# GEGLU feed-forward on one core: leading weights on one queue in 2 KB rows, later x behind chunk 5, chunks 6 and 7 by halves

## Chip, cores and metric

The kernel runs on one core of one Trainium2 chip. The metric is the device time of one execution in microseconds (us). Before the change three runs gave 299.56, 300.29 and 300.46 us, median 300.29.

## What is computed

From the reference, with x of 32 x 32 x 1024, w_gate and w_up of 1024 x 3584 and w_down of 3584 x 1024, all bf16:

```python
def _gelu(x):
    return jax.nn.gelu(x, approximate=True)
...
def reference(x, w_gate, w_up, w_down):
    return (_gelu(x @ w_gate) * (x @ w_up)) @ w_down
```

x is 1024 tokens of 1024 features. The first two products contract over features, the third over the 3584 hidden units.

## The kernel before

**Tiles and stages.** TensorE multiplies 128 x 128 weight tiles by up to 512 columns. The 1024 features are eight chunks of 128 (index k or dk), the hidden units 28 blocks of 128 (index m). A "part" is one block m for one range of tokens, with a gate sum G and an up sum U in PSUM, which has eight banks. Stage one makes all parts: TensorE sums G and U over the eight chunks (`part_step`, L362 to 392), ScalarE takes the gelu of G into a small buffer (L441, one of four), VectorE multiplies it by U into hT (L474; these multiplies are called E0, E1 and so on, by part). Stage two multiplies hT by w_down (L422), and ScalarE and VectorE by turns copy the result out, SyncE (SP) stores it.

**The start.** Weights and x come in together, and x has to be turned so that features lie on partitions. Tokens 0 to 255 (XA) arrive as two slices xa of 128 tokens, one on SP's queue and one on ScalarE's (L295). TensorE turns them by multiplying with an identity (`turn_xa`, L349 to 360; the identity is made on POOL, L319) into banks 3 to 7; four copies on VectorE and one on ScalarE (`xa_copy`, L302 to 307; `XA_PS` on L130 gives bank and chunks, `XA_ACT` on L131 the copies that are ScalarE's) bring them to xT. Tokens 256 to 1023 come later in three pieces: XB1 (128 tokens), XB2 (128) and XC2 (512) (`load_x`, L282 to 287; each piece by two queues, two transfers each, in 512-byte rows). VectorE turns them with its own transposes (L465): A0 to A7 are chunks of XB1, B of XB2, D of both together, C of XC2.

**Leading weights.** Blocks 0 to 7 of w_gate and w_up, 1024 columns, are needed first. `W0` (L134 to 136) cuts them: chunks 0 and 1 in two halves of 512 columns (1 KB rows), chunks 2 to 5 whole (2 KB rows), chunks 6 and 7 as a pair in two halves of 512 columns (1 KB rows). w_gate goes through SP's queue and w_up through ScalarE's (`early_loads`, L294 to 300), each behind its slice of xa and ahead of its half of later x. ScalarE makes its one xa copy after the ninth step of its issues (`ACT_EARLY`, L132). Each transfer has its own semaphore.

**The order by hand.** TensorE's order is a list of steps. `together` goes chunk by chunk over several parts, `one_by_one` finishes a part before the next; a step waits for its weights, for its bank to be free, for its xa copies or transposes. Parts 0 to 7 (blocks 0 to 7, tokens 0 to 255) and 8 to 15 (tokens 256 to 511) share a bank for G and U, so that ScalarE waits for U. The list at the start:

```python
together(range(0, 4), 0, 2)
together(range(4, 8), 0, 2)
together(range(0, 8), 2, 6)
one_by_one(range(0, 8), 6)
together(range(8, 12), 0, 4, XB1)
```

VectorE's order is the string `mix` (L190): multiplies E and transposes A to D. Part 8 reuses bank 0 and needs E0, part 11 needs E3. SP and POOL issue the later weights; their first such load waits for all of later x (`gate_w`, L309).

Of the kernel before, what the change touches and what calls it, by code (L numbers as in the profile page):

```python
# [5 lines left out]
P = 128  # L6
BF16 = mybir.dt.bfloat16
FP32 = mybir.dt.float32
ACTF = mybir.ActivationFunctionType
ALU = mybir.AluOpType  # L10
# [74 lines left out]
def bass_standalone__geglu_ffn__sampling_kernel(  # L85
# [13 lines left out]
    DK = D // P  # L99
# [7 lines left out]
    NBIG = 8  # L107
# [20 lines left out]
    XB1, XB2 = (256, 384), (384, 512)  # L128
    XPIECES = [XB1, XB2, XC2]
    XA_PS = [(3, 0, 1), (4, 1, 2), (5, 2, 4), (6, 4, 6), (7, 6, 8)]  # L130
    XA_ACT = (4,)  # L131
    ACT_EARLY = 9  # L132

    W0 = [(0, 1, 0, 512), (1, 2, 0, 512), (0, 1, 512, 1024), (1, 2, 512, 1024)]  # L134
    W0 += [(k, k + 1, 0, 1024) for k in range(2, 6)]
    W0 += [(6, 8, 0, 512), (6, 8, 512, 1024)]

    parts = []  # L140
# [22 lines left out]
    def together(ps_, k0, k1, tok=None):  # L163
        for dk in range(k0, k1):
            for key in ("G", "U"):
                for p in ps_:
                    steps.append((p, key, dk, tok))

    def one_by_one(ps_, k0):
        for p in ps_:  # L170
            for key in ("G", "U"):
                for dk in range(k0, DK):
                    steps.append((p, key, dk, None))

    for k0 in (0, 4):
        for b in range(2):
            steps += [("X", b, dk) for dk in range(k0, k0 + 4)]
    together(range(0, 4), 0, 2)
    together(range(4, 8), 0, 2)
    together(range(0, 8), 2, 6)  # L180
    one_by_one(range(0, 8), 6)
    together(range(8, 12), 0, 4, XB1)
    together(range(8, 12), 0, 4, XB2)
    together(range(8, 12), 4, 6)
# [2 lines left out]


    dve_order = []
    mix = ("E0 E1 E2 E3 A0 A1 A2 A3 B0 B1 B2 B3 E4 D4 D5 E5 D6 D7 E6 E7 "  # L190
           "C0 E8 C1 E9 C2 E10 E11 C3 C4 E12 C5 E13 C6 E14 C7 E15")
    for w in mix.split():
        if w[0] == "E":
            dve_order.append(("E", int(w[1:])))
# [13 lines left out]
    def evac_eng_is_act(ji):  # L208
        return ji % 2 == 0
# [11 lines left out]
    C_POOL = _Clock("pool")  # L221
    Q_XA = [_Clock(f"xa{b}", 16) for b in range(2)]
    Q_X = {(q, s): _Clock(f"x{i}{s}", 16) for i, q in enumerate(XPIECES) for s in range(2)}
    Q_W0 = {(w, p): _Clock(f"{w}0k{p[0]}c{p[2]}", 16) for p in W0 for w in ("wg", "wu")}
    Q_WG = [_Clock(f"wg{j}", 16) for j in range(NG)]
    Q_WU = [_Clock(f"wu{j}", 16) for j in range(NG)]
    Q_WD_SP = _Clock("wd_sp", 16)
# [1 line left out]
    Q_OUT = _Clock("out", 16)  # L229
    all_clocks = [C_PE, C_ACT, C_DVE, C_POOL, *Q_XA, *Q_X.values(), *Q_W0.values(), *Q_WG, *Q_WU,  # L230
                  Q_WD_SP, Q_WD_POOL, Q_OUT]

    ctx = _Ctx()

    with ExitStack() as es:
        def sb(name, shape, dtype):
            return es.enter_context(nc.sbuf_tensor(name, shape, dtype))
# [5 lines left out]
        xs = hT[:, FM - 8:FM, :].rearrange("p a (b e) -> p (a b) e", e=XE)  # L243
        xa = hT[:, FM - 10:FM - 8, :]
        ident = sb("ident", [P, P], BF16)
        big = {w: sb(w + "big", [P, DK, NBIG * P], BF16) for w in ("wg", "wu")}
        small = {w: sb(w + "small", [P, DK, GSZ * P], BF16) for w in ("wg", "wu")}
        w_r = {"wg": wg_r, "wu": wu_r}
# [10 lines left out]
        ones_w = nc.const_aps.tensor(1.0, [P, P], BF16)  # L259
# [22 lines left out]
        def load_x(ew, eng, q, side):  # L282
            c0, c1 = q[0] // 32, q[1] // 32
            for a in (2 * side, 2 * side + 1):
                v = ew.do(lambda: eng.dma_start(
                    xs[32 * a:32 * (a + 1), c0:c1, :], x_r[a, :, c0:c1, :]), clock=Q_X[(q, side)])
            ctx.set(("x", q, side), v)

        def load_w0(ew, eng, w, p):
            k0, k1, f0, f1 = p  # L290
            ctx.set((w + "0", p), ew.do(lambda: eng.dma_start(  # L291
                big[w][:, k0:k1, f0:f1], w_r[w][:, k0:k1, f0:f1]), clock=Q_W0[(w, p)]))

        def early_loads(ew, eng, side):  # L294
            yield ctx.set(("xa", side), ew.do(lambda: eng.dma_start(  # L295
                xa[:, side, :], xa_r[:, side, :]), clock=Q_XA[side]))
            for p in W0:
                yield load_w0(ew, eng, ("wg", "wu")[side], p)
            for q in XPIECES:
                yield load_x(ew, eng, q, side)  # L300

        def xa_copy(ew, j, copy):  # L302
            bank, k0, k1 = XA_PS[j]
            ew.wait(C_PE, ctx.get(("XP", j)))
            ctx.set(("XA", j), ew.do(lambda: copy(  # L305
                xT[:, k0:k1, XA[0]:XA[1]],
                ps[:, bank, 0:256 * (k1 - k0)].rearrange("p (k t) -> p k t", t=256))))

        def gate_w(ew, j):  # L309
            if war[j] is None:  # L310
                for s in range(2):
                    ew.wait(Q_X[(XC2, s)], ctx.get(("x", XC2, s)))
                return -1
            ew.wait(C_PE, ctx.get(("U", last_part[war[j]])))
            return war[j]

        def prog_pool(eng):
            pool = _Eng(ctx, eng, C_POOL)
            ctx.set("ident", pool.do(lambda: eng.affine_select(  # L319
                ident[:, :], ones_w, pattern=[[-1, P]], compare_op=ALU.is_equal,  # L320
                fill=0.0, base=0, channel_multiplier=1)))
            wd_mine = [k for k in range(len(wd_groups)) if k % 2 == 1]
            for j in range(NG):
                known_chunk = gate_w(pool, j)
                load_w(pool, eng, "wu", j)
                issue_wd(pool, eng, wd_mine, known_chunk, Q_WD_POOL)
            issue_wd(pool, eng, wd_mine, FM, Q_WD_POOL, force=True)
            ctx.set("wd_pool_total", Q_WD_POOL.n)
# [33 lines left out]
        def part_step(pe, eng, opened, i, key, dk, tok):  # L362
            m, t0, t1, gs, us = parts[i]
            w, (bank, f0, f1) = ("wg", gs) if key == "G" else ("wu", us)
            if tok is not None:
                f0, f1 = f0 + tok[0] - t0, f0 + tok[1] - t0
                t0, t1 = tok
            buf, slot, j = slot_of[m]
            if j is None:
                p = next(p for p in W0 if p[0] <= dk < p[1] and p[2] <= m * P < p[3])  # L370
                pe.wait(Q_W0[(w, p)], ctx.get((w + "0", p)))
            else:
                pe.wait((Q_WG if w == "wg" else Q_WU)[j], ctx.get((w, j)))
            if bank in bank_before[i]:
                pe.wait(C_DVE, ctx.get(("D", bank_before[i][bank])))
            for jx, (xbank, k0, k1) in enumerate(XA_PS):
                if t0 == XA[0] and (xbank == bank or k0 <= dk < k1):
                    pe.wait(C_ACT if jx in XA_ACT else C_DVE, ctx.get(("XA", jx)))
            for q in XPIECES:
                if q[0] < t1 and t0 < q[1]:  # L380
                    pe.wait(C_DVE, ctx.get(("T", dk, q)))
            first = (i, bank) not in opened
            opened.add((i, bank))
            last = (dk == DK - 1)
            v = pe.do(lambda: eng.matmul(  # L385
                ps[:, bank, f0:f1],
                wbuf(w, buf)[:, dk, slot * P:(slot + 1) * P],
                xT[:, dk, t0:t1],
                start=first, stop=last and (key == "U" or gs[0] != us[0]),
            ), mark=last)  # L390
            if last:
                ctx.set((key, i), v)
# [37 lines left out]
        def prog_act(eng):  # L430
            act = _Eng(ctx, eng, C_ACT)
            act.do(lambda: eng.activation(warm[:, 0:1], const0, ACTF.Gelu_apprx_tanh))  # L432
            for n, _ in enumerate(early_loads(act, eng, 1)):
                if n == ACT_EARLY - 1:
                    for j in XA_ACT:
                        xa_copy(act, j, lambda o, i: eng.activation(o, i, ACTF.Copy))
            for i, (m, t0, t1, (gb, g0, g1), us) in enumerate(parts):
                act.wait(C_PE, ctx.get(("U" if us[0] == gb else "G", i)))
                if i >= NTB:
                    act.wait(C_DVE, ctx.get(("D", i - NTB)))  # L440
                ctx.set(("A", i), act.do(lambda: eng.activation(  # L441
                    t_bufs[i % NTB][:, 0:t1 - t0], ps[:, gb, g0:g1], ACTF.Gelu_apprx_tanh)))
            for ji, (tc, col0, ncols, b) in enumerate(jobs):
                if not evac_eng_is_act(ji):
                    continue
                act.wait(C_PE, ctx.get(("O", ji)))
                ctx.set(("E", ji), act.do(lambda: eng.activation(  # L447
                    osb[:, tc, col0:col0 + ncols], ps[:, b, 0:ncols], ACTF.Copy)))

        def prog_dve(eng):  # L450
            dve = _Eng(ctx, eng, C_DVE)

            for j in range(len(XA_PS)):
                if j not in XA_ACT:
                    xa_copy(dve, j, eng.tensor_copy)
# [76 lines left out]
```

## Time and profile before

| What | us |
|---|---|
| median of 3 runs | 300.29 |
| the profiled execution's own time | 300.05 |
| its span (first to last instruction) | 298.8 |
| TensorE busy (matmuls) | 295.5 |
| VectorE busy | 58.4 |
| ScalarE busy | 42.0 |
| first slice of x issued on SP | 0.81 |
| first transposing matmul | 4.11 |
| first weight matmul | 5.21 |
| first gelu | 16.84 |
| stage two begins | 199.97 |
| last store issued | 297.18 |

The page shows the span in 40 slices of about 7.5 us, with each engine's busy share in tenths. A busy TensorE there need not be at its peak: matmuls are pipelined, so their lengths overlap, and the spacing of their starts is the measure. "Idle before" in the lists names the wait that ended last. An L and a number is a line of the kernel; PEld is TensorE's weight load, SPq, ACTq and POOLq are instructions that issue a transfer. q1 is the transfer queue of SP, q10 that of ScalarE, q0 that of POOL. The granted clock of TensorE is 1.00 in the whole execution.

### The profile page before, as it was taken

The numbers are of one execution on the slowest core, as the hardware profiler recorded it, in microseconds if no ns is written. First come the engines' busy times: TensorE is split into PE (matmuls) and PEld (weight loads), VectorE is DVE, ScalarE is ACT, GpSimd is POOL, SyncE is SP. The second block draws the span as 40 slices with busy tenths as digits, with TensorE's granted clock in tenths as the row PEclk, the third lists the DMA queues.
The fourth block names the chain that finished last, engine by engine and source line by source line (L and its number), as shares of the span: only waits on it lengthen the run. The fifth ranks groups of instructions, "written<-read, shape, count | busy, mean of one in ns | idle before, by whom it ended". The sixth has DMA issues, their size and how long they took to land.

```text
span 298.8 us, 3516 instructions
## 1 busy us (share of the span) xinstructions
PE 295.5 (99%) x1558; PEld 149.0 (50%) x1558; DVE 58.4 (20%) x96; ACT 42.0 (14%) x76; POOL 7.3 (2%) x13
## 2 busy tenths in 40 slices
PE   8999999999999999999999999999999999999997
PEld 5899644444444444444444444444444444444456
DVE  2069722111112111112211112210000000000000
ACT  2042211112111112111112111110000000000000
POOL 0001001020001002001000000000000000000000
DMA  7997103856008301942103000000000100010001
GB/s 229 376 240 245 41 1 116 307 176 247 0 0 282 141 0 24 371 169 97 46 0 140 0 2 0 0 0 20 18 18 20 35 18 18 20 35 18 18 20 35
DMA packets 18894, 26.43 MB, mean 88 GB/s; under 512 B 1088, under 2 KB 13504, under 8 KB 18880
## 3 DMA queue, kind: packets, MB, share of 16 engines
q1 hardware_dynamic: 13232, 14.68, 15.0%
q0 software_dynamic: 2176, 8.39, 7.7%
q10 hardware_dynamic: 3472, 3.15, 3.4%
q8 instruction: 12, 0.20, 0.3%
q14 instruction: 2, 0.02, 0.0%
HBM read 24.12 MB, written 2.10 MB: 88 GB/s over the span
## 4 chain that ended last, share of the span: by engine, by line
PE 96%; DMA 2%; SPq 1%; issue 0%; ACT 0%
PE ps L385 64%; PE ps L422 32%; DMA wgbig<-in_w_gate_dram 2%; SPq L291 1%; SPq L295 0%; ACT xT L447 0%
## 5 line engine op out<-in xcount | busy, mean ns | idle before, releaser
L422 PE MATMUL ps<-wd,hT 128*128 128x512 bf16 (+1 forms) x476 | 96.9, 366 | 0.0
L385 PE MATMUL ps<-xT,wgbig 128*128 128x512 bf16 (+2 forms) x400 | 80.2, 336 | 0.3 <-DMA wgbig<-in_w_gate_dram 0.2
L385 PE MATMUL ps<-xT,wubig 128*128 128x512 bf16 (+2 forms) x400 | 80.1, 336 | 0.0
L422 PEld LDWEIGHTS ps<-wd,hT 128*128 128x128 bf16 x476 | 46.6, 98 | 50.4
L474 DVE TENSOR_TENSOR hT<-tb,ps 128x512 bf16<-128x512 f32 (+1 forms) x64 | 39.2, 615 | 142.8 <-PE ps L385 142.6
L441 ACT ACTIVATE tb<-ps 128x512 f32<-128x512 f32 (+1 forms) x64 | 34.8, 544 | 158.0 <-PE ps L385 156.1
L385 PEld LDWEIGHTS ps<-xT,wgbig 128*128 128x128 bf16 x400 | 37.8, 98 | 32.6 <-DMA wgbig<-in_w_gate_dram 0.7
L385 PEld LDWEIGHTS ps<-xT,wubig 128*128 128x128 bf16 x400 | 38.1, 98 | 31.4
L385 PE MATMUL ps<-xT,wusmall 128*128 128x512 bf16 x128 | 30.2, 379 | 0.0
L385 PE MATMUL ps<-xT,wgsmall 128*128 128x512 bf16 x128 | 30.2, 379 | 0.0
L480 DVE CAST xT<-ps 128x512 bf16<-128x512 f32 (+1 forms) x8 | 5.3, 658 | 88.1 <-PE ps L422 88.1
L385 PEld LDWEIGHTS ps<-xT,wgsmall 128*128 128x128 bf16 x128 | 12.5, 98 | 15.1
L385 PEld LDWEIGHTS ps<-xT,wusmall 128*128 128x128 bf16 x128 | 12.5, 98 | 15.1
L447 ACT ACTIVATE xT<-ps 128x512 bf16<-128x512 f32 (+1 forms) x9 | 5.2, 573 | 93.1 <-PE ps L422 93.1
L465 DVE STREAM_TRANSPOSE xT<-hT 128x128 bf16<-128x128 bf16 (+2 forms) x20 | 13.4, 706 | 0.3 <-DMA hT<-in_x_dram 0.3
L279 POOL DMA_DIRECT2D wubig<-in_w_up_dram x3 | 2.6, 883 | 63.4 <-PE ps L385 63.4
L399 PE MATMUL ps<-const-bfloat16-1.0 128*128 128x512 bf16 (+1 forms) x10 | 3.1, 496 | 0.8 <-PEq L517 0.8
L279 POOL DMA_DIRECT2D wusmall<-in_w_up_dram x2 | 1.9, 971 | 48.4 <-PE ps L385 26.0
L305 DVE CAST xT<-ps 128x256 bf16<-128x256 f32 (+1 forms) x4 | 2.0, 550 | 4.6 <-PE ps L355 4.6
L273 POOL DMA_DIRECT2D wd<-in_w_down_dram x3 | 2.3, 761 | 19.1 <-PE ps L385 19.1
L399 PEld LDWEIGHTS ps<-const-bfloat16-1.0 128*128 128x128 bf16 x10 | 1.3, 142 | 2.5 <-issue 2.5
L432 ACT ACT_TABLE_LOAD x1 | 1.3, 1283 | 0.8 <-PEq L517 0.8
(9 smaller groups left out, 3.7 us busy)
## 6 DMA issues: line engine op xcount, KB each, us to landing
wd<-in_w_down_dram SPq DMA_DIRECT2D x4, 1024.0 KB, 11.4
wgbig<-in_w_gate_dram SPq DMA_DIRECT2D x3, 1024.0 KB, 5.5
wubig<-in_w_up_dram POOLq DMA_DIRECT2D x3, 1024.0 KB, 9.6
wd<-in_w_down_dram POOLq DMA_DIRECT2D x3, 1024.0 KB, 11.2
wgsmall<-in_w_gate_dram SPq DMA_DIRECT2D x2, 1024.0 KB, 5.5
wusmall<-in_w_up_dram POOLq DMA_DIRECT2D x2, 1024.0 KB, 9.4
out_dram<-xT SPq DMA_DIRECT2D x15, 128.0 KB, 1.7
wgbig<-in_w_gate_dram SPq DMA_DIRECT2D x6, 256.0 KB, 8.2
```

What stands on the lines that cost most here:

```text
L273: ew.do(lambda: eng.dma_start(wd[:, a:b, :], wd_r[:, a:b, :]), clock=clock)
L279: ctx.set((w, j), ew.do(lambda: eng.dma_start(wbuf(w, buf)[:, :, 0:gsz * P], w_r[w][:, :, c0 * P:(c0 + gsz) * P]), clock=q))
L291: ctx.set((w + "0", p), ew.do(lambda: eng.dma_start(big[w][:, k0:k1, f0:f1], w_r[w][:, k0:k1, f0:f1]), clock=Q_W0[(w, p)]))
L305: ctx.set(("XA", j), ew.do(lambda: copy(xT[:, k0:k1, XA[0]:XA[1]], ps[:, bank, 0:256 * (k1 - k0)].rearrange("p (k t) -> p k t", t=256))))
L385: v = pe.do(lambda: eng.matmul(ps[:, bank, f0:f1], wbuf(w, buf)[:, dk, slot * P:(slot + 1) * P], xT[:, dk, t0:t1], start=first, stop=last ...
L399: pe.do(lambda: eng.matmul(ps[:, 0, 0:n], ones_w, ones_x[:, 0:n], start=True, stop=True), mark=False)
L422: v = pe.do(lambda: eng.matmul(ps[:, b, 0:ncols], hT[:, m, tc * P:(tc + 1) * P], wd[:, m, col0:col0 + ncols], start=(m == 0), stop=(m == F ...
L441: ctx.set(("A", i), act.do(lambda: eng.activation(t_bufs[i % NTB][:, 0:t1 - t0], ps[:, gb, g0:g1], ACTF.Gelu_apprx_tanh)))
L447: ctx.set(("E", ji), act.do(lambda: eng.activation(osb[:, tc, col0:col0 + ncols], ps[:, b, 0:ncols], ACTF.Copy)))
L465: v = dve.do(lambda: eng.transpose(xT[:, dk, q[0]:q[1]].rearrange("p (c i) -> p c i", i=32), src))
L474: ctx.set(("D", i), dve.do(lambda: eng.tensor_tensor(hT[:, m, t0:t1], t_bufs[i % NTB][:, 0:t1 - t0], ps[:, ub, u0:u1], ALU.mult)))
L480: ctx.set(("E", ji), dve.do(lambda: eng.tensor_copy(osb[:, tc, col0:col0 + ncols], ps[:, b, 0:ncols])))
```

## The change

- The cut `W0` goes. Each chunk of blocks 0 to 7 is one transfer per weight, 128 rows of 2 KB. All sixteen are issued on SP's queue, w_gate and w_up by turns, chunk by chunk.
- ScalarE issues its slice of xa, makes two xa copies (chunk 1 and chunks 6 to 7) instead of one, waits for the landing of chunk 5 of w_up, and then issues its half of later x. SP issues its half behind the weights, as before.
- TensorE's order: chunk 0 for parts 0 to 3, then for 4, 7, 5, 6; chunks 1 to 5 for all eight; then chunk 6 for four parts together and chunk 7 part by part, first for parts 0 to 3, then 4 to 7.
- VectorE: A0 stands ahead of E3, and C7 ahead of E14.
- The identity is made by an iota, a wait and a compare on POOL instead of one select.

```diff
-    XA_ACT = (4,)
-    ACT_EARLY = 9
-
-    W0 = [(0, 1, 0, 512), (1, 2, 0, 512), (0, 1, 512, 1024), (1, 2, 512, 1024)]
-    W0 += [(k, k + 1, 0, 1024) for k in range(2, 6)]
-    W0 += [(6, 8, 0, 512), (6, 8, 512, 1024)]
-
+    XA_ACT = (1, 4)
...
-    together(range(0, 4), 0, 2)
-    together(range(4, 8), 0, 2)
-    together(range(0, 8), 2, 6)
-    one_by_one(range(0, 8), 6)
+    together(range(0, 4), 0, 1)
+    together((4, 7, 5, 6), 0, 1)
+    together(range(0, 8), 1, 6)
+    for half in (range(0, 4), range(4, 8)):
+        together(half, 6, 7)
+        one_by_one(half, 7)
...
-    mix = ("E0 E1 E2 E3 A0 A1 A2 A3 B0 B1 B2 B3 E4 D4 D5 E5 D6 D7 E6 E7 "
-           "C0 E8 C1 E9 C2 E10 E11 C3 C4 E12 C5 E13 C6 E14 C7 E15")
+    mix = ("E0 E1 E2 A0 E3 A1 A2 A3 B0 B1 B2 B3 E4 D4 D5 E5 D6 D7 E6 E7 "
+           "C0 E8 C1 E9 C2 E10 E11 C3 C4 E12 C5 E13 C6 C7 E14 E15")
...
-        def load_w0(ew, eng, w, p):
-            k0, k1, f0, f1 = p
-            ctx.set((w + "0", p), ew.do(lambda: eng.dma_start(
-                big[w][:, k0:k1, f0:f1], w_r[w][:, k0:k1, f0:f1]), clock=Q_W0[(w, p)]))
+        def load_w0(ew, eng, w, k):
+            ctx.set((w + "0", k), ew.do(lambda: eng.dma_start(
+                big[w][:, k, :], w_r[w][:, k, 0:NBIG * P]), clock=Q_W0[(w, k)]))
 
         def early_loads(ew, eng, side):
-            yield ctx.set(("xa", side), ew.do(lambda: eng.dma_start(
+            ctx.set(("xa", side), ew.do(lambda: eng.dma_start(
                 xa[:, side, :], xa_r[:, side, :]), clock=Q_XA[side]))
-            for p in W0:
-                yield load_w0(ew, eng, ("wg", "wu")[side], p)
+            yield
+            if side == 0:
+                for k in range(DK):
+                    for w in ("wg", "wu"):
+                        load_w0(ew, eng, w, k)
+            else:
+                ew.wait(Q_W0[("wu", 5)], ctx.get(("wu0", 5)))
             for q in XPIECES:
-                yield load_x(ew, eng, q, side)
+                load_x(ew, eng, q, side)
...
-            ctx.set("ident", pool.do(lambda: eng.affine_select(
-                ident[:, :], ones_w, pattern=[[-1, P]], compare_op=ALU.is_equal,
-                fill=0.0, base=0, channel_multiplier=1)))
+            v = pool.do(lambda: eng.iota(diff[:, :], pattern=[[1, P]], base=0, channel_multiplier=-1))
+            pool.wait(C_POOL, v)
+            ctx.set("ident", pool.do(lambda: eng.tensor_scalar(
+                ident[:, :], diff[:, :], 0.0, None, ALU.is_equal)))
...
-            for n, _ in enumerate(early_loads(act, eng, 1)):
-                if n == ACT_EARLY - 1:
-                    for j in XA_ACT:
-                        xa_copy(act, j, lambda o, i: eng.activation(o, i, ACTF.Copy))
+            for _ in early_loads(act, eng, 1):
+                for j in XA_ACT:
+                    xa_copy(act, j, lambda o, i: eng.activation(o, i, ACTF.Copy))
```

More of the change, by code (lines that the diff above doesn't have):

```diff
@@ L223, in bass_standalone__geglu_ffn__sampling_kernel @@
     Q_X = {(q, s): _Clock(f"x{i}{s}", 16) for i, q in enumerate(XPIECES) for s in range(2)}
-    Q_W0 = {(w, p): _Clock(f"{w}0k{p[0]}c{p[2]}", 16) for p in W0 for w in ("wg", "wu")}
+    Q_W0 = {(w, k): _Clock(f"{w}0k{k}", 16) for k in range(DK) for w in ("wg", "wu")}
     Q_WG = [_Clock(f"wg{j}", 16) for j in range(NG)]
@@ L245, in bass_standalone__geglu_ffn__sampling_kernel @@
         ident = sb("ident", [P, P], BF16)
+        diff = sb("diff", [P, P], mybir.dt.int32)
         big = {w: sb(w + "big", [P, DK, NBIG * P], BF16) for w in ("wg", "wu")}
@@ L369, in part_step @@
             if j is None:
-                p = next(p for p in W0 if p[0] <= dk < p[1] and p[2] <= m * P < p[3])
-                pe.wait(Q_W0[(w, p)], ctx.get((w + "0", p)))
+                pe.wait(Q_W0[(w, dk)], ctx.get((w + "0", dk)))
             else:
```

## The prediction

> **What bounds the kernel now.** I read the page's slices first: TensorE is busy from end to end, the DMA engines hardly matter after the first fifth.
>
> ```profile
> PE   8999999999999999999999999999999999999997
> ...
> DMA  7997103856008301942103000000000100010001
> ```
>
> So a change of the start is worth only TensorE's idle time in it. The waits of the weight-load rows (PEld; a matmul cannot start before its load) name three suspects besides the first arrival of x:
>
> ```profile
> PEld ps L385 <- DMA wgbig<-in_w_gate_dram: 0.7, 2, 0.5
> PEld ps L385 <- DVE xT L465: 0.7, 2, 0.5
> ...
> DVE xT L465 <- DMA hT<-in_x_dram: 0.3, 1, 0.3
> ```
>
> These rows overstate the loss, since a matmul already in flight covers part of a late load. The timeline gives the exact size, because matmuls of one shape start at a fixed pace. Columns: start, length, engine, line, operation, count.
>
> ```profile
> 5.65 0.60 PE L385 MATMUL ps<-xT,wubig 128*128 128x256 bf16 x4
> 6.17 0.61 PE L385 MATMUL ps<-xT,wgbig 128*128 128x256 bf16 x4
> ...
> 8.36 0.60 PE L385 MATMUL ps<-xT,wubig 128*128 128x256 bf16 x4
> 9.21 1.05 PE L385 MATMUL ps<-xT,wgbig 128*128 128x256 bf16 x8 [0.24 <-DMA wgbig<-in_w_gate_dram]
> 10.09 1.04 PE L385 MATMUL ps<-xT,wubig 128*128 128x256 bf16 x8
> ...
> 19.48 0.38 PE L385 MATMUL ps<-xT,wubig 128*128 128x256 bf16 x2
> 19.81 0.38 PE L385 MATMUL ps<-xT,wgbig 128*128 128x128 bf16 x4
> ...
> 33.86 2.08 PE L385 MATMUL ps<-xT,wgbig 128*128 128x512 bf16 x8
> ```
>
> Eight matmuls of 256 columns take 0.87 us (9.21 to 10.09), so one takes 0.109. Four from 5.65 should hand over at 6.09, and the next is at 6.17: 0.08 lost (chunk 1). Four from 8.36 hand over at 8.80, next 9.21: 0.41 lost (chunk 2, w_gate). Two from 19.48 hand over at 19.70, next 19.81: 0.11 lost (the first transpose of later x, itself waiting for x until 19.25). The eight from 33.86 take 2.08 where a later set of the same shape takes 1.89: 0.19 lost (the last transpose C7, behind the multiply E14). **Sum 0.79 us.** Everything else until 296.8 is matmul after matmul, at clock 1.00.
>
> Behind the first three lies the rate at which 6 MB arrive, by stretch (last columns: clock, share of the 16 DMA engines, GB/s):
>
> ```profile
> 5.00:6.00 1.00, 1.00 (x13) 0.85 (x11) 1.00 (x4) 0.52 (x1) 0.00 (x0) 1.00 0.95 302
> ...
> 10.00:11.00 1.00, 1.00 (x12) 0.90 (x10) 0.00 (x0) 0.00 (x0) 0.00 (x0) 1.00 1.05 406
> ...
> 13.00:14.00 1.00, 1.00 (x11) 0.90 (x10) 0.00 (x0) 0.00 (x0) 0.00 (x0) 1.00 1.10 351
> ```
>
> The engines are full in all three; what differs is the row: 1 KB in 5 to 6 and 13 to 14, 2 KB in 10 to 11. Chunk 2's w_gate row, late by 0.41, stands behind 1 MB of 1 KB rows.
>
> **Part by part.** The sum goes against the profiled execution: span 298.8, its time 300.05, which is 0.24 under the median of the three runs (300.29).
>
> *The base.* If all four losses go and nothing comes, 300.05 - 0.79 = 299.26. What is late next decides.
>
> *One queue, 2 KB rows, in TensorE's order.* SP issues 17 loads instead of 11 before x. Its ten weight issues took 5.04 us, 0.50 each, so sixteen end at 1.25 + 8.1 = 9.3; at 400 GB/s 256 KB takes 0.66, so the issue keeps ahead. TensorE eats 256 KB in eight matmuls, 0.87 us. Whether a queue alone is as fast as two is seen late in the trace, where SP's queue brings 2 KB rows of w_down by itself, in 160.5 to 162.5:
>
> ```profile
> DMA packets 389, 0.80 MB, mean 398 GB/s; under 512 B 0, under 2 KB 0, under 8 KB 389
> ...
> q1 hardware_dynamic: 389, 0.80, 103.0%
> ```
>
> That is one large load, not sixteen after each other; the gap g between loads on a lone queue is not in the trace. Below it is bounded by 0; above by 0.67: chunk 3 and 4 of w_gate landed 10.5 and 11.9 (issue plus time to landing), 1.35 apart on a queue that shared with another, and all that is not its own 0.66 could hide a gap. I take 0, from the row with the lone queue. The Trainium skill ("DMA: Bandwidth & Descriptors", Anatomy of one DMA) says the semaphore write behind a load costs about a cycle, which is g = 0 also; no row here isolates it.
>
> Landings then: the first w_gate half landed at 4.65 (1.25 + 3.4) behind both first slices of x; the whole 256 KB should be there between 4.7 and 5.0, before the 5.21 at which the first matmul starts. The first w_up row follows 0.67 later if the stretch runs at 400, at up to 6.48 if one DMA engine is as far behind as now (the same number of bytes stands before the second w_up half of now: 1.77 + 4.7). It is due 0.44 after the start. So 0 to 0.75 is lost there; with 0.9 us per row, the 300 GB/s of now, it is **0.25**, which I take, as the nearest stretch in time. The later rows come faster than 0.87 apart: nothing lost, the 0.08 and 0.41 go.
>
> *The second slice of x.* ScalarE's slice (xa 1) landed at 4.25 (0.86 + 3.4), and TensorE's four transposes that need it started just 0.13 later, without slack: the first copy, and with it the first matmul at 5.21, hang on it. Packets of two queues alternate, so each of its remaining 2 KB packets now waits behind one of 2 KB instead of 1 KB. By the trace's packet records some 93 such packets were left at 3 us, and at full rate a packet of 1 KB takes 46 ns, one of 2 KB 84 ns: 93 x 38 ns over 16 engines is 0.22; part of those alternate with xa 0 anyway. I take **+0.14**, bounds 0 and 0.25.
>
> *Copies and bank order.* ScalarE's copy for bank 4 (256 columns, by its 384 ns gelu row) runs beside VectorE's first; order 4, 7, 5, 6 meets bank 7 at 5.35 + 0.98 = 6.33, where the copy (5.48 to 6.08 now, plus its handover) is ready, and bank 6 at 6.55, with VectorE's third copy ending near 6.4. Cost 0; if ScalarE's two copies ran late, 0.1 each.
>
> *Identity.* iota, a wait and a compare stand in place of one 0.28 us select on POOL at 0.90. Neither is in the trace. Below 0; above, the longest POOL row is 0.97: two of these end at 2.9, and TensorE needs it at 4.11. Cost 0, hidden by the arrival of x.
>
> *Later x.* ScalarE now waits for chunk 5 of w_up (landed 13.7 now; 12.8 with 1 MB at 400 instead of 300) and issues six loads in 4.2 us, to 17.0. Queued behind are its gelus. The first was possible 0.31 after part 0's last up matmul started; with chunks 6 and 7 by halves that is the tenth matmul after chunk 6 begins (S), not the fourth: S + 0.98 + 0.31. S is 5.21 + 96 x 0.109 = 15.68, plus my 0.39: 16.07. The gelu is due 17.36: 0.3 of cover. VectorE's E2 then starts at S + 2.5, A0 at S + 2.8; A0 to first matmul is 0.56 now (19.25 to 19.81), so S + 3.36, before the 32 matmuls end (S + 3.49). E3 follows A0 and frees bank 3 at S + 3.65, due S + 3.66. Chunk 7's last row lands 4 x 0.67 after chunk 5, 15.5, to 16.0 with ScalarE's x beside it; a 16 KB instruction packet (one in 15.5 to 16.6 now; of the two last w_up and w_gate pieces one landed at 18.06, the other at 16.43) can hold it on one engine to 17.1; due S + 0.98 = 17.05. First later x: SP's side behind chunk 7, 16.4 to 18.0, due 18.8. The 0.11 goes; the three near misses together **+0.10**, bounds 0 and 0.5.
>
> *C7 ahead of E14.* C7 starts one 0.30 multiply earlier, the loss was 0.19: gone.
>
> Sum: 300.05 - 0.79 + 0.25 + 0.14 + 0.10 = 299.75, **299.7**.
>
> **Rivals.** (1) *Everything lands in time:* the lone queue runs at 400 from the start and xa 1 is not held. For: 398 alone; against: 300 in the first 4 us now, with no more than row size to blame. 299.26 to 299.4. (2) *The lone queue has gaps,* the slower side: it decides from g = 0.2, where 0.67 + g reaches TensorE's 0.87. At g = 0.3 the sixteenth row lands at 4.65 + 15 x 0.97 = 19.2, due 16.8: 2.4 late; 300.05 - 0.79 + 0.14 + 2.4 = 301.8. For: two queues cover each other now; against: the 398 of a load whose rows have no gap. (3) *Identity late:* it must come after 4.11, over 3.2 us after 0.90. With the trace's longest one-time load (ACT_TABLE_LOAD, 1.28) before each of two 0.28 operations and a 0.2 wait: 4.2, 0.1 late. The Trainium skill ("GPSIMD Engine Reference", Instruction dispatch) puts the first call into freshly loaded code at about 6 us, which would be an estimated 303; the select row with its configuration steps at 0.8 paid none. (4) *The rows do not do what they say:* the slow first 4 us are not a matter of 1 KB rows. Then w_up's first row costs the full 0.75 and the late end 0.5: 300.05 - 0.79 + 0.75 + 0.14 + 0.5 = 300.65.
>
> **Numbers.** A difference under about 0.3% (0.9 us) cannot be told from no change. Forecast 52% (299.4 to 300.3), rival 1 25% (more than 0.3% under 300.29 is 299.39), rival 2 14%, rival 3 4%, rival 4 5%. Faster 0.25 (rival 1); same 0.58 (forecast, rival 4, and 1% of rival 3); slower 0.17 (rival 2 and 3% of rival 3). Range 299.2 to 301.0: it leaves out the larger part of rival 2, rival 3's long case, and a little below.
>
> **What would show it.** Right: first matmul near 5.35, a handover loss of about 0.25 at the first w_up matmul, none at chunk 2, none near 33; stretches 5 to 12 near 400 GB/s on one queue. Wrong: chunk landings over 0.87 apart (rival 2); transposes on POOL (rival 3); ScalarE's first gelu after its last issue rather than after TensorE, or a wait at the first 128-column matmul.

## The result and the profile after

The changed kernel takes 302.13 us (median of 6 runs, 301.38 to 302.54), the kernel before 300.15 in the same comparison (6 runs, 299.56 to 300.46): 1.0067 times, interval 1.0049 to 1.0084. It is slower by 2.0 us, where 299.7 was forecast and the range ended at 301.0. The profiled execution took 302.44, its span 301.1 against 298.8.

The timeline of TensorE in the changed kernel (start, length, engine, line, operation, count, wait) holds the whole loss:

```profile
15.73 0.60 PE L386 MATMUL ps<-xT,wgbig 128*128 128x256 bf16 x4
16.17 0.60 PE L386 MATMUL ps<-xT,wubig 128*128 128x256 bf16 x4
16.60 0.27 PE L386 MATMUL ps<-xT,wgbig 128*128 128x256 bf16 x1
18.20 0.28 PE L386 MATMUL ps<-xT,wubig 128*128 128x256 bf16 x1 [1.32 <-DMA wubig<-in_w_up_dram]
...
20.61 0.27 PE L386 MATMUL ps<-xT,wubig 128*128 128x256 bf16 x1
22.25 0.44 PE L386 MATMUL ps<-xT,wgbig 128*128 128x128 bf16 x4 [1.37 <-DVE xT L465]
```

Up to 16.6 there is no loss any more: the four at 15.73 stand 0.44 ahead of the next four, chunk after chunk. Then the first matmul of chunk 7 of w_up is 1.49 us late (16.60 + 0.11 to 18.20), and the first on later x 1.53 late (20.61 + 0.11 to 22.25). Before, the first matmul on later x ran at 19.81, now at 22.25, 2.44 later; the loss at C7 (0.19) is gone; the difference of the two, 2.25, is the 2.3 of the spans. VectorE says what it waited for ahead of its first transpose, A0 (engine, line, cause; total, times, longest):

```profile
DVE xT L465 <- DMA hT<-in_x_dram: 1.7, 1, 1.7
```

ScalarE's row of issues in the timeline of the changed kernel (start, length, what, count):

```profile
12.93 3.64 ACTq L282 DMA_DIRECT2D hT<-in_x_dram  x6
```

The transfers of the changed kernel in the stretch from 14.5 to 17.9 (packets, MB, rate; then by queue: packets, MB, share; q1 is SP's):

```profile
DMA packets 1265, 0.67 MB, mean 196 GB/s; under 512 B 83, under 2 KB 1226, under 8 KB 1265
...
q1 hardware_dynamic: 1265, 0.67, 122.2%
```

The same by queue from 19.5 to 21.5 (q10 is ScalarE's):

```profile
q10 hardware_dynamic: 815, 0.40, 116.5%
q1 hardware_dynamic: 54, 0.03, 7.5%
```

ScalarE asked for its x from 12.93 on, as expected. In the 3.4 us from 14.5 not one packet of it moved; only SP's queue did. Its first x packet is at 18.01 in the packet records, 5.1 us after the first issue, when SP's queue had moved 4969 KB of the 5120 KB that SP had asked for before 12.93 (its first slice of x, 4096 KB of weights, 768 KB of later x). The second of ScalarE's two blocks of the first piece landed at 21.6 (13.29 + 8.3), and A0 began at 21.71. And while only SP's side moved, the rate was 190 GB/s; before, with both, it was 291 (engines' busy times, then clock, DMA share, GB/s):

```profile
18.00:19.00 1.00, 1.00 (x12) 0.87 (x10) 0.96 (x3) 0.87 (x3) 0.00 (x0) 1.00 1.20 291
```

The line above is the kernel before; the next one is the changed kernel, where the two sides move at different times, with the DMA engines just as full (share 1.23):

```profile
17.00:18.00 1.00, 0.00 (x0) 0.00 (x0) 0.00 (x0) 0.00 (x0) 0.00 (x0) 1.00 1.23 190
```

**Theory.** Transfers of SP and of ScalarE are served nearly in the order in which they were asked for, over both queues. SP asked for its x right behind the weights (9.13 to 12.49), ScalarE after a landing, so ScalarE's side had to stand behind all of SP's. **Rivals:** ScalarE's x is late because of its own wait alone; SP's queue always goes first; a lone queue is slow with short rows; the late chunk 7 is the cause.

### The profile page after: what moved, and what is told of

The parts are those of the page before. It is cut to its first block, busy times and chain, and to the rows that moved or that the text cites. A ratio compares the mean times of both kernels' runs of the same rounds, so it can differ in the third digit from the quotient of the medians.

```text
span 301.1 us, 3511 instructions
## 1 busy us (share of the span) xinstructions
PE 295.3 (98%) x1558; PEld 149.2 (50%) x1558; DVE 57.7 (19%) x95; ACT 41.9 (14%) x77; POOL 7.9 (3%) x14
## 2 busy tenths in 40 slices
DMA packets 17806, 26.43 MB, mean 88 GB/s; under 512 B 1024, under 2 KB 11392, under 8 KB 17792
## 4 chain that ended last, share of the span: by engine, by line
PE 92%; DMA 5%; SPq 2%; issue 0%; DVE 0%; ACT 0%; ACTq 0%; DVEq 0%
PE ps L386 60%; PE ps L423 32%; DMA hT<-in_x_dram 3%; DMA wubig<-in_w_up_dram 2%; SPq L287 2%; DVE xT L465 0%; SPq L291 0%; ACT xT L447 0%; ACTq L282 0%; DVEq L41 0%
## 5 line engine op out<-in xcount | busy, mean ns | idle before, releaser
L480 DVE CAST xT<-ps 128x512 bf16<-128x512 f32 (+1 forms) x8 | 5.3, 658 | 88.1 <-PE ps L423 88.1
L306 DVE CAST xT<-ps 128x512 bf16<-128x512 f32 (+1 forms) x3 | 1.6, 595 | 4.7 <-PE ps L357 4.7
L357 PE MATMUL ps<-ident,hT 128*128 128x128 bf16 x16 | 1.3, 231 | 0.3 <-DMA hT<-in_x_dram 0.3
```

The costliest lines, as they stand in the source:

```text
L306: ctx.set(("XA", j), ew.do(lambda: copy(xT[:, k0:k1, XA[0]:XA[1]], ps[:, bank, 0:256 * (k1 - k0)].rearrange("p (k t) -> p k t", t=256))))
L480: ctx.set(("E", ji), dve.do(lambda: eng.tensor_copy(osb[:, tc, col0:col0 + ncols], ps[:, b, 0:ncols])))
```

## The experiments

Unless another kernel is named, an edit is made to the changed kernel. Times are medians beside runs of the kernel before on the same chip; ratios are to that.

**1. Both queues on one half of the partitions** (in the kernel before).

```diff
-            for a in (2 * side, 2 * side + 1):
+            for a in (side, side + 2):
```

> The kernel before, with one line changed: both queues bring the x blocks of partitions 0 to 63 first, then both those of 64 to 127 (before, one queue had the lower half and the other the upper half at the same time). Theory (each half of the partitions can take only about 200 GB/s, so the change lost rate because its two sides of x came one after the other): the stretch of later x falls from 290 to about 200 GB/s, the last x lands near 25 instead of 22.9, the first transpose starts 0.3 to 1 us later than 19.25, time 300.3 to 301. Rival (a queue alone is slow with 512-byte rows, whichever partitions it writes): both queues still run together, 290 GB/s, no change of time.

Time 299.94, ratio 1.0011 (0.9996 to 1.0027). Both queues moved at once, and still:

```profile
18.00:19.00 1.00, 1.00 (x12) 0.90 (x10) 0.91 (x4) 0.84 (x4) 0.00 (x0) 1.00 1.21 202
```

202 GB/s, not 291, with two queues in both cases: the rate goes with which partitions are written, not with the number of queues. (The columns of x that are read side by side change with the edit too; no run separates that.) The Trainium skill ("SBUF — State Buffer", Door 1: The DMA port swizzle) says that partitions 0 to 63 reach only 8 of 16 ports, about 196 GB/s for a large load; the run agrees. The expected loss of time did not come: the last x landed near 23.6, but in this execution the weights happened to come without the early waits, and the first piece of x landed at 18.5, in time. So the rate is real, and it is not by itself the 2 us.

**2. SP's x behind chunk 5 too.**

```diff
-            else:
-                ew.wait(Q_W0[("wu", 5)], ctx.get(("wu0", 5)))
+            ew.wait(Q_W0[("wu", 5)], ctx.get(("wu0", 5)))
```

> The changed kernel, with SP holding its side of later x back until chunk 5 of w_up has landed, as ScalarE does. Theory (ScalarE's issued x did not move for 5 us because its requests stood behind SP's unfinished x): both sides move within 1.5 us of their issue and together, x at about 290 GB/s once the weights are in, the first x piece lands by 18.5, the wait of 1.5 us at the first later-x matmul falls under 0.4, time about 300.7; the wait for chunk 7 of w_up (1.5 us) stays or shrinks a little. Rival (ScalarE's x is late because of its own wait alone): its x still moves only from 18 on, and nothing is gained.

299.82, ratio 1.0002 (0.9992 to 1.0011): the whole loss is gone. ScalarE asks at 12.81, much as in the change, and its first packet moves at 14.36, when SP's queue had moved 4278 KB of the 4352 KB asked for earlier: this time only the weights stand in front. In the timeline the chunk 7 wait is still there, the later-x wait is not:

```profile
16.53 0.27 PE L385 MATMUL ps<-xT,wgbig 128*128 128x256 bf16 x1
17.55 0.28 PE L385 MATMUL ps<-xT,wubig 128*128 128x256 bf16 x1 [0.75 <-DMA wubig<-in_w_up_dram]
...
19.96 0.27 PE L385 MATMUL ps<-xT,wubig 128*128 128x256 bf16 x1
20.07 0.39 PE L385 MATMUL ps<-xT,wgbig 128*128 128x128 bf16 x4
```

19.96 + 0.11 is 20.07: no wait. ScalarE's own wait is untouched, so it is not the cause by itself; that it stood behind SP's x is. Only the time was forecast too high (300.7).

**3. ScalarE does not wait.**

```diff
-            else:
-                ew.wait(Q_W0[("wu", 5)], ctx.get(("wu0", 5)))
```

> The changed kernel, with ScalarE issuing its side of later x right behind its two copies, without the wait for chunk 5. Theory (a request stands behind unfinished ones of the other queue, and packets of two queues alternate): ScalarE's x moves from about 7.5 us and is in by 14; the weights give up to 0.8 MB of room to it and run near 0.87 us per 256 KB, so 0 to 1 us of waits in chunks 2 to 5, w_up chunk 7 lands between 17 and 18.5; the first later x then waits for SP's side alone, 18 to 19. Time 300 to 301.5. Rival (ScalarE's late issue is all that was wrong, and the weights are not slowed): under 300.3, with only the wait for chunk 7 left.

302.73, ratio 1.0103 (1.0074 to 1.0133), more than the theory or the rival gave. ScalarE asked from 5.46 on, and its first x packet moved at 9.04, when SP's queue had moved 2242 KB of the 2560 KB asked for earlier: the order of asking again, now behind weights. ScalarE's first block landed at 11.60, ahead of weights that SP asked for after it (at 5.75, landed at 13.42): so SP's queue does not always go first. From there x took room from the weights, and losses for late weights run from 7.0 to 19.75, about 3.0 us in all (chunk 7 landed at 19.70). The wait in the change keeps this away; what it costs depends on what SP has asked for by then.

**4. Both behind chunk 7.**

```diff
-                ew.wait(Q_W0[("wu", 5)], ctx.get(("wu0", 5)))
+            ew.wait(Q_W0[("wu", 7)], ctx.get(("wu0", 7)))
```

> The changed kernel, with both sides of later x held back until chunk 7 of w_up has landed, so that no x moves beside the weights. Theory (the 512-byte x packets of the other engines made the last weight packets of the engine that was behind take 160 ns instead of 84): chunk 7 of w_up lands near 16.8 instead of 18.15, its wait is under 0.3 us; x starts near 18 and its first piece lands near 19.8, so 0.8 to 1.5 us are lost at the first later-x matmul. Time 300.2 to 301. Rival (the 16 KB instruction packet alone delays chunk 7): it lands at 17.8 or later and its wait stays over 1 us.

301.55, ratio 1.0073 (1.0045 to 1.01). Chunk 7 of w_up landed at 16.60 and was used without a wait, as the theory had it. The first matmul on later x came 2.13 us late, but the wait was not for x, whose first piece landed at 19.45 (ScalarE's rows of the timeline, then VectorE's):

```profile
16.62 2.84 ACTq L282 DMA_DIRECT2D hT<-in_x_dram  x6
19.51 2.04 ACT L440 ACTIVATE tb<-ps 128x256 f32<-128x256 f32 x7 [13.45 <-PE ps L385]
...
19.93 1.08 DVE L473 TENSOR_TENSOR hT<-tb,ps 128x256 bf16<-128x256 f32 x3 [13.51 <-ACT tb L440]
20.93 0.40 DVE L464 STREAM_TRANSPOSE xT<-hT 128x128 bf16<-128x128 bf16 x1
```

ScalarE's gelus stood behind its six issues, which ended at 19.46; part 0 had been summed by 17.10. E0 to E2 came after the gelus and A0 after E2, at 20.93, 1.48 us after its x was there. This is the sign of error that the prediction named, ScalarE's first gelu after its last issue rather than after TensorE; in the change itself the issues ended at 16.57 and the first gelu, at 18.52, waited for TensorE. So this run's time says nothing against or for the order of asking. In its profiled execution (303.24) TensorE's clock also halved for a while (last section); the three other runs, 301.54 to 301.56, kept the full clock.

**5. Both behind chunk 6.** As 2, with 6 in place of 5.

> The changed kernel, with both sides of later x held back until chunk 6 of w_up has landed (14.2 to 14.4). Theory (x packets beside the weights of the engine that the instruction packet holds up make chunk 7 late, and both sides of x move at once when their requests are made at once): x moves from 15.4, chunk 7 of w_up lands between 16.6 and 17.2 (17.5 with chunk 5 as the gate, 16.6 with chunk 7), its wait is under 0.5 us; the first piece of x lands by 18.6, the wait there is under 0.4. Time 299.2 to 299.7, 0.1% to 0.3% under the kernel before. Rival (chunk 7 is late by the instruction packet alone on the run's luck): its wait stays near 0.9 and the time at 299.8 or above.

299.91, ratio 0.9992 (0.9974 to 1.001), not the gain that was expected. The first piece of x was in time (18.3). Chunk 7 landed at 17.64, as late as with the chunk 5 gate, and its wait was 0.62. The theory on chunk 7 missed: its w_gate row was already 1.6 us behind on one DMA engine, and had been held up by the instruction packet at 14.1, before x began at 15.5.

**6. As 2, without the halves.**

```diff
-    for half in (range(0, 4), range(4, 8)):
-        together(half, 6, 7)
-        one_by_one(half, 7)
+    one_by_one(range(0, 8), 6)
```

> As with both sides behind chunk 5, but chunks 6 and 7 part by part as in the kernel before, without the halves. Theory (the halves move the first use of chunk 7 of w_up from the fourth to the tenth matmul of chunk 6, 0.65 us later): the wait for chunk 7 grows from 0.9 by 0.65 us, to about 1.6, time 300.4. Rival (the waits are set by x and the halves are worth nothing or cost the handover to VectorE): no change from 299.8.

300.12, ratio 1.0000 (0.9989 to 1.0011). Chunk 7 landed at 16.39 this time, its wait was 0.34, and the first later-x matmul had none; the expected wait of 1.6 and time of 300.4 did not come. The halves are worth less than these runs can tell, because the landing of chunk 7 varies by more than the 0.65 us that they move its use.

**7. Only SP's last piece behind chunk 5.**

```diff
+                if side == 0 and q == XC2:
+                    ew.wait(Q_W0[("wu", 5)], ctx.get(("wu0", 5)))
                 load_x(ew, eng, q, side)
```

> The changed kernel, with only SP's last and largest x piece held back until chunk 5 of w_up has landed; its first two pieces go out behind the weights as in the change, and ScalarE waits for chunk 5. Theory (requests of both queues are served nearly in the order in which they were made, whichever queue they are on): ScalarE's first x packet moves when SP's 4608 KB made before it are nearly through, at 15 to 16, not at 18.0; the first-x wait falls from 1.5 to under 0.5 us; time 299.8 to 300.5. Rival (any x of SP ahead of it holds ScalarE's back until SP's side has ended): first packet at 17.5 or later.

301.93, ratio 1.0061 (1.0041 to 1.008). The first packet came at 15.91, when SP's queue had moved 4670 KB, just past the 4608 KB asked for earlier, as the order of asking has it and not as the rival. But the gain did not follow: ScalarE's second block, asked for at 13.16, stood by the order of asking behind SP's two large blocks (12.75 and 13.10), released by the same landing. It landed at 21.5, and the first later-x matmul ran at 22.16. A piece is as late as its last block.

**8 and 9. The last chunks, then also chunk 0, by columns.** As 2, with chunks 6 and 7 cut as in the kernel before, on SP's queue (the lines that follow from the new pieces are left out):

```diff
+    W0 = [(k, k + 1, 0, 1024) for k in range(6)]
+    W0 += [(6, 8, 0, 512), (6, 8, 512, 1024)]
```

9 replaces the first entry by `(0, 1, 0, 512), (0, 1, 512, 1024)`.

> As with both sides of x behind chunk 5, and the last two chunks cut as in the kernel before (both chunks, 512 columns, then the other 512), still on SP's queue alone. Theory (what is left is the wait for chunk 7 of w_up, whose last packets sit on the engine that the instruction packet holds up; blocks 0 to 3 then have all their rows two transfers earlier and blocks 4 to 7 have 1.75 us more): the wait for chunk 7 (0.9) falls to 0 to 0.2, only the 0.2 to 0.45 at the first w_up row is left. Time 299.2 to 299.7. Rival (1 KB rows cost rate on this queue, or the lag is longer than that cover): the chunk 7 wait stays above 0.5, 299.8 or more.

> As the one before, and chunk 0 cut by columns too, so that the first w_up matmuls need 128 KB and not 256. Theory (the first w_up row is late only because the whole rows of both weights stand in front of it): the wait at the first w_up matmul (0.2 to 0.45) goes to under 0.1; time 299.0 to 299.5, the best of all, 0.2% to 0.35% under the kernel before. Rival (the first 4 us are slow whatever the rows): the wait moves to blocks 4 to 7 of chunk 0 or to chunk 1, and the time equals the one before.

8: 299.88, ratio 0.9989 (0.9975 to 1.0002). 9: 300.5, ratio 1.001 (0.9998 to 1.0023). In 8 the wait for chunk 7 is gone, as expected; the profiled execution lost about 1.0 at the start instead, because TensorE ran the transposing and the first weight matmuls at half pace until 6.6 (four matmuls of 256 columns from 5.77 to 6.62; chunk 1 began at 8.01, and 5.21 + 1.75 would be 6.96). In 9 the wait moved from the first w_up row to chunk 1 (0.47), as its rival had it, chunk 7 of blocks 4 to 7 was late by 0.19 and the first later x by 0.32. Neither can be told from the kernel before.

**10. ScalarE's wait alone, in the kernel before.**

```diff
+            if side == 1:
+                ew.wait(Q_W0[("wu", (5, 6, 0, 1024))], ctx.get(("wu0", (5, 6, 0, 1024))))
             for q in XPIECES:
                 yield load_x(ew, eng, q, side)
```

> The kernel before, weights on two queues as they were, with one thing of the change: ScalarE waits for chunk 5 of w_up ahead of its side of later x. Theory (requests are served nearly in the order made, over both queues): ScalarE's x, made at 13.3, stands behind all of SP's x, made by 10.3; its first packet moves at 16.5 to 18 instead of 15.4 and its first piece lands at 20.5 to 21.5; first-x wait 1 to 2 us where it was 0.11; time 301 to 302. Rival (each queue has its own share of the engines at all times): its x moves 1.1 us after its issue, at 14.5 to 15, first piece by 18.5, no loss.

303.46, ratio 1.0096 (1.0068 to 1.0124). With the weights on two queues as they were, ScalarE's x was asked for at 14.59 and first moved at 18.38, when SP's queue had moved 2933 KB of the 3072 KB asked for earlier; its first piece landed at 22.89. The waits of the profiled execution:

```profile
PEld ps L387 <- DVE xT L467: 3.8, 2, 3.3
...
DVE xT L467 <- DMA hT<-in_x_dram: 2.9, 1, 2.9
```

The later-x wait grew from 0.11 to 3.17 us, part of it because chunk 5 landed 0.9 us later here. Two of the four runs, 304.02 and the profiled 306.54, also had stretches at half clock (last section); the two at full clock, 302.02 and 302.9, are 2.0 and 2.8 us over the kernel before. This one edit is enough for the loss, with no lone queue, no 2 KB row and no halves.

**11 and 12. One more execution each** of experiment 4 and of the changed kernel, beside one of the kernel before, which took 301.2; their value is in the timelines, not in the times.

> A second look at the kernel with both sides of x behind chunk 7 of w_up, for the spread. If x beside the last weights is part of what makes chunk 7 late: it lands again by 17.0 and is used without a wait (16.6 before). If the instruction packet and chance do it alone: it may land anywhere from 16.4 to 18.2, as in the kernels with x beside it.

> A second look at the changed kernel, for the spread. If x beside the last weights is part of it: chunk 7 of w_up lands again at 17.7 or later (18.15 before) and its wait is over 0.9 us; ScalarE's first x packet again comes when SP's x is nearly through, 17.5 to 18.5, and the first later-x matmul waits 1.3 us or more. If chance rules: chunk 7 can be as early as 16.4.

11: 301.48, chunk 7 landed at 16.39, and again ScalarE's issues, to 19.25, held up its gelus (first at 19.30), not x (landed at 19.15). 12: 302.01, and its chunk 7 landed at 16.04, without a wait; the span was 300.7. The waits of 12:

```profile
PEld ps L386 <- DVE xT L465: 2.3, 2, 2.1
PEld ps L386 <- DMA wubig<-in_w_up_dram: 0.9, 1, 0.9
```

The one for w_up is now the first row of the kernel (0.82 late), and nothing is lost at chunk 7. Yet the first later-x matmul comes at 21.82, 2.01 later than in the profile of the kernel before. So the late chunk 7 is not the cause of the 2 us: what TensorE does not wait there it waits at the first later x, whose time ScalarE's x sets (first packet 17.66, landed 21.18).

## Why the prediction was wrong, point by point

- **The base held.** The four losses (0.08, 0.41, 0.11, 0.19) were what there was to gain, and in the first profile of the change those of chunks 1 and 2 and of C7 went.
- **The lone queue held, g is about 0.** From 12 to 14 the changed kernel's transfers, on q1 alone and one 256 KB transfer after the other, ran at 407 GB/s; rival 2 is out:

```profile
DMA packets 438, 0.81 MB, mean 407 GB/s; under 512 B 48, under 2 KB 48, under 8 KB 437
...
q1 hardware_dynamic: 437, 0.80, 104.0%
```

  The rate was less even than the sign asked for, 328 GB/s from 5 to 6 and 365 to 391 in the stretches from 6 to 12, but in this profile no landing was late for it before chunk 7. From 6 to 8 it was 391 and 387, against 306 and 281 with the 1 KB rows of before, so rival 4 is not borne out as a whole.
- **The first w_up row** was put at 0.25: 0 in the first profile, 0.82 in the second, 0.17 in experiment 2. The size is that of a spread.
- **The second slice of x** was put at +0.14. It landed at 4.3 (0.79 + 3.5) instead of 4.25, and the first weight matmul ran at 5.25 instead of 5.21: 0.04 (in the second profile it ran at 5.05). Two copies and the identity cost nothing: iota 0.23 and compare 0.54 had ended by 1.7. Rival 3 is out.
- **The failed step is "Later x": it timed the first piece by SP's side alone.** It counted ScalarE's issue rightly (12.8 to 17.0; it was 12.93 to 16.57), but gave no landing for ScalarE's side and took SP's, behind chunk 7, as the last, 16.4 to 18.0, due 18.8. SP's first piece landed at 18.84, 0.8 past that estimate; ScalarE's at 21.6. The step had no row for a transfer that is asked for beside a queue with much in front. In place of that, the runs show service nearly in the order of asking: ScalarE's first packet moved when SP's queue had moved 97% of what was asked for earlier in the change, 88% in experiment 3, 98% in 2 and 95% in 10.
- **The size of that term.** The +0.10, at most 0.5, stood for three near misses. In the first profile chunk 7 cost 1.49 (it landed at 18.15, where 17.1 was the latest expected) and later x 1.53, together 3.02; in the second chunk 7 cost nothing and later x 1.97. With the measured terms the sum comes out: 300.05 - 0.79 + 0.04 + 3.02 = 302.32, where the profiled execution took 302.44.
- **No rival was this mechanism.** The text named "ScalarE's first gelu after its last issue" and "a wait at the first 128-column matmul" as signs of an error; the second is what came. Rival 1 fell with the late landings. The slower rival's 301.8 is near the measured time by chance: it needs gaps between the loads, and there were none.
- The Trainium skill ("DMA: Bandwidth & Descriptors", Queues, rings and completion order) has each DMA engine take turns between the queues that have work for it. Once both queues move, the trace agrees: in the kernel before, 602 packets of q1 and 600 of q10 moved from 17 to 19. It does not contradict the order of asking if ScalarE's transfers become work for the engines late; why they would is open, since the runs show only that their packets are absent.

**What stays open:** what in the chip keeps the order of asking, and why chunk 7 of w_up lands anywhere between 16.04 and 18.15 in two executions of one kernel. An instruction packet of 16 KB takes 1.0 to 1.4 us on one engine near that time in every execution, and the last weight packet ended between 15.3 and 16.8 (experiment 3, with x in front, apart). From there to the landing it took 0.44 and 0.49 us in the two executions with no x beside it (4 and 11) and 0.7 to 1.5 in those with x beside rows of 2 KB, 1.47 and 0.73 in the two of the change: x beside it goes with up to 1 us, and what sets its share is not settled.

## What to carry to other kernels

Two issuing engines are two places in one line: before a transfer is held back on one queue, count what the other has already asked for, since that is served first, and hold both back together or neither. Count also what else waits behind the issues on the engine that makes them: in experiment 4 six issues held up ScalarE's gelus, and with them all that followed. Take the landing of a piece as that of its last block, and for the rate let transfers to both halves of the partitions move at the same time. When two waits follow each other, ask when the last of them would end without the first; only that one is worth mending.

## What the runs showed of the hardware that was not expected

Later x moved at 291 GB/s with partitions 0 to 63 and 64 to 127 written at once, and at 190 to 202 with one half at a time, with the engines' busy share at 1.2 either way: a full share is not a full rate. And TensorE's granted clock fell to 0.50 after a wait of 2.13 us in the profiled execution of experiment 4, for 3.4 us, and after one of 3.17 us in that of experiment 10, for 6.8 us, while 1.97 us (the second execution of the change) and 1.84 us (the second execution of experiment 4) left it as it was. The stretch after it, in experiment 4 (the last three columns are clock, DMA share and GB/s):

```profile
22.00:23.00 1.00, 1.00 (x12) 1.00 (x11) 1.00 (x4) 0.11 (x1) 0.00 (x0) 0.50 1.22 242
```

So such a wait was dearer than its own length. From the first later-x matmul to the end of the span, experiment 4 took 280.4 us (21.47 to 301.9) and the second execution of the change 278.9 (21.82 to 300.7), 1.5 less; experiment 10 took 281.8 (23.53 to 305.3), 2.9 more than that. These are single executions, so no threshold is shown.
